# Attention followed by a token mixer: load pieces, a projection's period, the order of the drain and the last store are changed

## The chip, the cores and the metric

The kernel runs on one core of a Trainium2 chip. A core has a matrix engine (TensorE, PE in the profile; PEld is its loading of weights), a vector engine (VectorE, DVE), a scalar engine (ScalarE, ACT), a general one (GpSimd, POOL) and a queue engine (SyncE, SP), which run their own instruction streams in order and wait for each other by semaphores. PE writes to PSUM, an accumulation memory from which DVE or ACT must copy results ("evict" them) to SBUF, the working memory. Sixteen DMA engines move data between HBM (device memory) and SBUF; here POOL issues all loads, which convert float32 to float16 on the way, and SP issues all stores. The metric is the device time of one execution in microseconds, lower is better.

## The reference

```python
def _attn_ref(q, k, v):                  # 8 batches, 8 heads, 576 tokens, head_dim 64
    q_c = q.reshape(B, H, nc, chunk, D)  # chunks of 64 tokens, nc = 9; k_c, v_c alike
    scores = scale * np.matmul(q_c, k_c.transpose(0, 1, 2, 4, 3))
    scores = scores - np.max(scores, axis=-1, keepdims=True)
    attn = np.exp(scores)
    attn = attn / (np.sum(attn, axis=-1, keepdims=True) + 1e-09)
    out = np.matmul(attn, v_c)
...
def _moe_ref(x, w_q, w_k, w_out):        # x: 8 x 576 x 512, the heads side by side
    wq = x @ w_q                         # w_q, w_k: 512 x 64
    wk = x @ w_k
    W_tok = scale * np.einsum('bsd,btd->bst', wq, wk)
    mixed = np.einsum('bst,btd->bsd', W_tok, x)
    return (np.maximum(mixed, 0.0) @ w_out).astype(np.float32)   # w_out: 512 x 512
```

Attention works inside chunks of 64 tokens, so each batch has 72 independent 64 x 64 softmaxes. Its result x goes through a mixer without a softmax, which the kernel computes as wq (wk^T x), so that the token-by-token matrix is never built.

## The kernel before, in words

**Loads.** `load(b, cuts)` fills, for one batch, two tiles `qn` (q and k, 128 partitions x 2 halves of the heads x 9 tiles of tokens) and one tile `vt`. With `cuts` as `None` it issues three DMAs: q, k and v whole, 576 KB each as float16 (L89 to L99). With cuts it issues, for each range of tiles, q in two halves, k in two halves and v in two halves (L100 to L107). Batch 0 is cut in three ranges (18 DMAs, L110), batch 1 in two (12 DMAs, L121). On POOL's queue the projection weights `wqk16` (four DMAs) stand between batch 0 and batch 1, and `wout16` (two DMAs) between batch 1 and batch 2; batches 2 to 5 follow. Batches 6 and 7 are issued from inside the loop when buffers are free.

**Attention.** The 72 chunks of a batch are worked in groups of eight, called units here; 36 units cover the 8 batches, 4.5 units per batch. Unit u goes through stages: `stage_a1` transposes q and k of load tiles 2u and 2u+1 on PE (16 transposes into the one buffer of PSUM tile `tp`, L327); `stage_a2` copies them to `qkt` on DVE (L337); `stage_b1` multiplies q by k (`sp`, L351) and takes the maximum (`mx`, L359); `stage_b2` subtracts it on DVE (`sh`, L365) and takes the exponential on ACT (`es`, L373); `stage_c` transposes that on PE (`ep`, L380) and copies it on ACT (`et`, L382); `stage_d1` multiplies by v (`xp`, L395); `stage_d2` normalises on DVE into `x_nat` (L410).

The order is written out by hand. Period `kk` of the main loop (L453 to L473) issues b1(kk), d1(kk-2), then filler work of place 0, a1(kk+2), filler of place 1, c(kk-1), b2(kk), d2(kk-2), a2(kk+2), filler of place 2. So a1 runs two periods ahead, and every engine meets the work in this order. Before the loop, a1 and a2 of units 0 and 1 are issued.

**The mixer as filler.** `make_moe(b)` makes the steps of batch b. `xts[0..2]` transpose x (six transposes, tile `tx`, L143) and evict them on ACT into `xt` (L150; for the last batch the third is shared by DVE and ACT, L147 and L148). `p_wqk(0)` and `p_wqk(1)` multiply by both projections (`wpa`, `wpb`, L163 and L166; the second also evicts to `wqkT` on ACT, L173 and L174, and copies half of it with DVE, L176). `p_wkn` transposes wk (`wknp`, L190) and evicts it (L195). `p_g` makes wk^T x (`gp`, L205 and L209; evicted on ACT, L213). `p_mixed(0)`, `p_mixed(1)` and `p_mixed_tail` multiply by wq (`ma`, `mb`, L225 and L245) and evict with the ReLU into `rmx` (L131 on ACT; for half of the last batch L129 on DVE). `p_out(0..3)` multiply 128 tokens each by w_out (`op`, four matmuls, L261), evict to `osb` (L269) and store 256 KB through SP (L270); `p_out_tail` does the last 64 tokens (`opt`, eight matmuls, L281, evicted on ACT, L289, and stored in two DMAs, L291). All of these PSUM tiles rotate through the same three buffers.

**The plan.** Each step of `chain` (L298 to L307) is a row (periods after the batch's last unit, place, cost, wait, step). `plan` puts it in that period and place. In a place, `fill` runs the planned steps and then takes ready out steps from `outs` in their order as long as the cost fits a budget (0.7 in place 1, 1.4 or 1.9 in place 2). A batch's outs become ready when its whole chain has run. What the loop does not reach is the drain (L475 to L488): `last` holds the steps of batch 7, `rest` those of earlier batches. It walks both lists with a clock of costs: the next step of batch 7 is issued when `wait` has passed on that clock since the step before it, or nothing else is left; otherwise a step of `rest` or of `outs` is issued. The costs and waits are only numbers that order the instructions; the chip does not see them.

Of the kernel before, what the change touches and what calls it, by code (L numbers as in the profile page):

```python
# [17 lines left out]
def kernel(  # L18
# [15 lines left out]
    nc = tc.nc  # L34
    B, H, S, D = q.shape
    DM = moe_w_out.shape[0]
    DH = moe_w_q.shape[1]
    CH = 64
    P = 128
# [9 lines left out]
    ds = bass.ds  # L49
# [27 lines left out]
    def load(b, cuts):  # L77
        qn = [
            qn_pool.tile([P, 2, NT, R * D], F16, name=f"qn{ti}", tag=f"qn{ti}")
            for ti in range(2)  # L80
        ]
        vt = v_pool.tile([P, 2, NS, D + 2], F16, name="vt", tag="vt")
        flat = [
            x[b].rearrange("h s d -> (h s) d").rearrange("(l t p r) d -> l p t (r d)", l=2, p=P, r=R)
            for x in (q, k)
        ]
        vflat = v[b].rearrange("h s d -> (h s) d").rearrange("(l n p) d -> l p n d", l=2, p=P)
        nc.gpsimd.memset(vt[:, :, :, D : D + 1], 1.0)
        if cuts is None:  # L89
            for ti in range(2):  # L90
                nc.gpsimd.dma_start(
                    qn[ti][:].rearrange("p l t e -> p (l t) e"),
                    flat[ti].rearrange("l p t e -> p l t e").rearrange("p l t e -> p (l t) e"),
                )
            nc.gpsimd.dma_start(  # L95
                vt[:].rearrange("p l n e -> p (l n) e")[:, :, 0:D],
                vflat.rearrange("l p n d -> p l n d").rearrange("p l n d -> p (l n) d"),
            )
            return qn, vt  # L99
        for t0, t1 in cuts:  # L100
            for ti in range(2):
                for sl in range(2):
                    nc.gpsimd.dma_start(qn[ti][:, sl, t0:t1, :], flat[ti][sl, :, t0:t1, :])  # L103
            for sl in range(2):
                nc.gpsimd.dma_start(  # L105
                    vt[:, sl, 2 * t0 : 2 * t1, 0:D], vflat[sl, :, 2 * t0 : 2 * t1, :]
                )  # L107
        return qn, vt

    loads = [load(0, [(0, 2), (2, 5), (5, 9)])]  # L110
    wqk16 = const.tile([P, HQ, 2 * DH], F16, name="wqk16")
    wout16 = const.tile([P, HQ, DM], F16, name="wout16")

    def w_rows(w):
        return w.rearrange("(l i d) j -> l d i j", l=2, i=HQ)

    for sl in range(2):
        rows = slice(CH * sl, CH * sl + CH)
        nc.gpsimd.dma_start(wqk16[rows, :, 0:DH], w_rows(moe_w_q)[sl])
        nc.gpsimd.dma_start(wqk16[rows, :, DH:], w_rows(moe_w_k)[sl])  # L120
    loads.append(load(1, [(0, 3), (3, 9)]))  # L121
    for sl in range(2):
        nc.gpsimd.dma_start(wout16[CH * sl : CH * sl + CH, :, :], w_rows(moe_w_out)[sl])
    for b in range(2, 6):
        loads.append(load(b, None))

    def relu(on_vector, to, of):
        if on_vector:
            nc.vector.tensor_scalar(to, of, scale_moe, 0.0, op0=ALU.mult, op1=ALU.max)  # L129
        else:  # L130
            nc.scalar.activation(to, of, AF.Relu, scale=scale_moe)  # L131

    def make_moe(b):
# [20 lines left out]
        def p_wqk(half):  # L154
            def run():
                xt = st["xt"]
                if half == 0:
                    st["pa"] = m_psum.tile([P, 512], F32, name="wpa", tag="m")
                    st["pb"] = m_psum.tile([P, CH], F32, name="wpb", tag="m")
                pa, pb = st["pa"], st["pb"]  # L160
                for i in (2 * half, 2 * half + 1):
                    flags = dict(start=(i == 0), stop=(i == HQ - 1))
                    nc.tensor.matmul(  # L163
                        pa[:, :], lhsT=wqk16[:, i, :], rhs=xt[:, NC_ * i : NC_ * i + 8, :], **flags
                    )
                    nc.tensor.matmul(  # L166
                        pb[:, :], lhsT=wqk16[:, i, :], rhs=xt[:, NC_ * i + 8, :], **flags
                    )
                if half == 0:
                    return  # L170
                wqkT = moe_pool.tile([P, S], F16, name="wqkT", tag="wqkT")
                wqd = moe_pool.tile([P, S], F16, name="wqd", tag="wqd")
                nc.scalar.copy(wqkT[:, 0:512], pa[:])  # L173
                (nc.vector.tensor_copy if b == B - 1 else nc.scalar.copy)(wqkT[:, 512:S], pb[:])  # L174

                nc.vector.tensor_copy(wqd[CH:P, :], wqkT[0:CH, :])  # L176
                st["wqkT"], st["wqd"] = wqkT, wqd

            return run
# [36 lines left out]
        def p_mixed(w):  # L216
            def run():
                if w == 0:
                    st["rmx"] = moe_pool.tile([P, HQ, S], F16, name="rmx", tag="rmx")
                g16, rmx = st["g16"], st["rmx"]  # L220
                wq = (st["wqkT"][0:CH], st["wqd"][CH:P])
                ms = []
                for par in range(2):
                    ma = m_psum.tile([P, 512], F32, name=f"ma{par}", tag="m")
                    nc.tensor.matmul(  # L225
                        ma[:], lhsT=g16[CH * par : CH * par + CH, w, :], rhs=wq[par][:, 0:512]
                    )
                    ms.append(ma)
                for par in range(2):

                    relu(
                        b == B - 1 and par == 1,
                        rmx[:, 2 * w + par, 0:512].rearrange("p (c g r) -> p c g r", g=G, r=R),
                        ms[par][:].rearrange("p (c r g) -> p c g r", g=G, r=R),
                    )

            return run
# [18 lines left out]
        def p_out(t):  # L256
            def run():
                rmx = st["rmx"]
                op = m_psum.tile([P, DM], F32, name="op", tag="m")
                for i in range(HQ):  # L260
                    nc.tensor.matmul(  # L261
                        op[:],
                        lhsT=rmx[:, i, ds(t * P, P)],
                        rhs=wout16[:, i, :],
                        start=(i == 0),
                        stop=(i == HQ - 1),
                    )
                osb = osb_pool.tile([P, DM], F32, name="osb", tag="osb")
                (nc.vector.tensor_copy if b == B - 1 and t % 2 else nc.scalar.copy)(osb[:], op[:])  # L269
                nc.sync.dma_start(out[b, ds(t * P, P), :], osb[:])  # L270

            return run

        def p_out_tail():
# [20 lines left out]
        xts = [p_xt(g) for g in range(3)]  # L295


        chain = [  # L298
            (1, 2, 0.4, 0.2, xts[2]),
            (1, 2, 0.5, 0.4, p_wqk(0)),  # L300
            (1, 2, 0.5, 0.0, p_wqk(1)),
            (2, 0, 0.4, 1.2, p_wkn),
            (3, 1, 0.7, 0.9, p_g),
            (4, 0, 0.25, 0.8, p_mixed(0)),
            (5, 0, 0.25, 0.8, p_mixed(1)),
            (5, 1, 0.15, 0.5, p_mixed_tail),
        ]  # L307
        outs = [(2, 0.9, p_out(t)) for t in range(4)]
        outs.append((1, 0.5, p_out_tail))
        return xts[:2], chain, outs  # L310

    def batch_of(gj):
# [2 lines left out]
    data = dict(enumerate(loads))  # L315
# [27 lines left out]
    def stage_b1(u):  # L343

        qkt = state[u]["qkt"]
        sp = s_psum.tile([P, 8, CH], F32, name="sp", tag="sp")
        for i in range(8):
            j, c = divmod(i, 4)
            for sl in range(2):
                rows = slice(CH * sl, CH * sl + CH)  # L350
                nc.tensor.matmul(  # L351
                    sp[rows, i, :],
                    lhsT=qkt[rows, j, 0, c, :],
                    rhs=qkt[rows, j, 1, c, :],
                    start=True,
                    stop=True,
                )
        mx = sm_pool.tile([P, 8], F32, name="mx", tag="mx")
        nc.vector.tensor_reduce(mx[:], sp[:], axis=AX.X, op=ALU.max)  # L359
        state[u]["sp"], state[u]["mx"] = sp, mx  # L360
# [72 lines left out]
    outs = []  # L433
# [19 lines left out]
    for kk in range(NU + 2):  # L453
        if kk < NU:
            stage_b1(kk)
        if kk >= 2:
            stage_d1(kk - 2)
        fill(kk, 0, 0.0)
        if kk + 2 < NU:
            stage_a1(kk + 2)  # L460
        fill(kk, 1, 0.7)
        if 1 <= kk <= NU:
            stage_c(kk - 1)
        if kk < NU:
            stage_b2(kk)
        if kk >= 2:
            stage_d2(kk - 2)
        if kk + 2 < NU:
            stage_a2(kk + 2)
        fill(kk, 2, 1.4 if len(outs) < 4 else 1.9)  # L470
        for b in range(B - 6):
            if 4 * (kk - 1) >= NS * (b + 1) > 4 * (kk - 2):
                data[b + 6] = load(b + 6, None)  # L473

    rest = [x for key in sorted(plan) for x in plan[key]]  # L475
    last = [x for x in rest if x[0] == B - 1]
# [40 lines left out]
```

## Time and profile before

| | |
|---|---|
| time, median of 3 runs | 179.73 us (178.91 to 181.5) |
| the profiled execution | 179.23 us |
| its span, first to last instruction | 177.5 us |
| share of that outside of the span | 1.7 us |
| mean granted TensorE clock | 0.98 |
| loads | 14.81 MB as float16, on the software queue |
| stores | 9.44 MB, on the hardware queue |

The profile is one execution. Its page gives for each engine the busy time with its share of the span and the number of instructions, and then the span in 40 equal slices of 4.4 us, one digit each, in tenths of a slice (9 means 90% or more). PEclk is the TensorE clock that was granted, in the same tenths, and DMA the mean busy share of the 16 DMA engines. Lists of waits give who waited for whom, with the total, the number of times and the longest. Timeline rows give start, duration, engine, line, operation, output and inputs, shape and count, and in brackets the idle time of the engine before and what ended it. In the rows that group instructions, what follows the bar is busy time, the mean of one in ns, and the idle time before with what ended it. In the rows of DMA issues, the last number is the time from issue to landing. Busy time of a PE that pipelines its matmuls is modelled and not the same as PE at its peak.

### The profile page before, as it was taken

Reading aid. Unit: us, or ns where it says so; the run is one execution under the profiler, and the core shown is the slowest. Engines: PE = TensorE matmul, PEld = TensorE weight load, DVE = VectorE, ACT = ScalarE, POOL = GpSimd, SP = SyncE. Lnnn points to the kernel's source line nnn. Section 1 sums busy time; section 2 is a strip of 40 time slices with the busy share of each in tenths; the row PEclk is TensorE's granted clock in tenths of the full one; section 3 lists DMA queues with packets and bytes.
Section 4 is the critical chain, followed back from the end, with each engine's and each line's share of the span. In section 5 each row is a group of like instructions: output and inputs, shape, how many; then the busy total and the mean of one; then the engine's idle time right before and its main releaser. Section 6 shows DMA issues by size and latency. Waiting matters only on the chain.

```text
span 177.5 us, 5756 instructions
## 1 busy us (share of the span) xinstructions
PE 140.1 (79%) x2496; PEld 92.2 (52%) x2496; DVE 113.8 (64%) x239; ACT 102.9 (58%) x203; POOL 55.2 (31%) x68
## 2 busy tenths in 40 slices
PE   0364987953977799997997999799979996798990
PEld 0241755842565566665574665566756654454440
DVE  0122869694199778956995988669959865731241
ACT  2001222540548867975797499747956986596630
POOL 8999999916343542422400000000000000000000
PEclk9999999995699999999999999999999999999999
DMA  2999999999999999999999992401303124032435
GB/s 28 98 120 145 112 123 159 185 183 168 177 176 168 182 164 209 231 203 252 178 195 223 173 226 80 151 2 63 94 4 118 60 77 136 0 122 89 177 121 177
DMA packets 82041, 24.62 MB, mean 139 GB/s; under 512 B 76384, under 2 KB 77920, under 8 KB 82016
## 3 DMA queue, kind: packets, MB, share of 16 engines
q0 software_dynamic: 76128, 14.81, 99.1%
q1 hardware_dynamic: 5888, 9.44, 15.5%
q8 instruction: 19, 0.31, 0.7%
q14 instruction: 6, 0.05, 0.1%
HBM read 29.62 MB, written 9.44 MB: 220 GB/s over the span
## 4 chain that ended last, share of the span: by engine, by line
PE 32%; ACT 28%; POOL 17%; DVE 10%; DMA 7%; issue 3%; ACTq 0%; POOLq 0%; DVEq 0%
PE op L261 11%; ACT rmx L131 9%; POOL qn L103 8%; DMA qn<-in_k_dram 7%; ACT xt L150 6%; ACT es L373 5%; POOL vt L105 5%; PE tp L327 4%; PE wpa L163 3%; PE xp L395 2%; ACT et L382 2%; PE ep L380 2%; DVE mx L359 2%; PE sp L351 2%; DVE sh L365 2%
## 5 line engine op out<-in xcount | busy, mean ns | idle before, releaser
L327 PE MATMUL tp<-ident,qn 128*64 128x128 f16 x576 | 30.8, 242 | 17.1 <-DMA qn<-in_q_dram 9.0
L382 ACT COPY et<-ep 128x512 f16<-128x512 f16 x36 | 21.2, 589 | 33.9 <-PE ep L380 33.8
L337 DVE COPY qkt<-tp 128x1024 f16<-128x1024 f16 x36 | 24.6, 682 | 19.1 <-PE tp L327 19.1
L327 PEld LDWEIGHTS <-qn 128*64 128x64 f16 x576 | 21.7, 120 | 25.5 <-DMA qn<-in_q_dram 10.4
L261 PE MATMUL op<-wout,rmx 128*128 128x512 f16 x128 | 31.2, 379 | 0.3 <-ACT xt L148 0.2
L373 ACT ACTIVATE es<-sh 128x512 f16<-128x512 f32 x36 | 22.9, 635 | 13.6 <-DVE sh L365 12.6
L359 DVE TENSOR_REDUCE mx<-sp 128x8 f32<-128x512 f32 x36 | 24.7, 687 | 8.9 <-PE sp L351 8.7
L365 DVE TENSOR_TENSOR sh<-sp,mx 128x512 f32<-128x512 f32 x36 | 24.8, 690 | 2.0
L410 DVE TENSOR_TENSOR x_nat<-xp,rec 128x512 f16<-128x512 f32 x36 | 24.9, 692 | 1.2
L269 ACT COPY osb<-op 128x512 f32<-128x512 f32 x30 | 17.4, 586 | 5.2 <-PE op L261 4.0
L395 PE MATMUL xp<-vt,et 64*64 64x65 f16 x576 | 16.2, 198 | 5.2 <-DVE x_nat L410 3.5
L351 PEld LDWEIGHTS <-qkt 64*64 64x64 f16 x576 | 12.8, 115 | 11.4 <-issue 6.6
L150 ACT COPY xt<-tx 128x768 f16<-128x768 f16 x23 | 18.3, 795 | 0.0
L351 PE MATMUL sp<-qkt 64*64 64x64 f16 x576 | 17.0, 203 | 0.8 <-DVE sh L365 0.8
L131 ACT ACTIVATE rmx<-ma 128x512 f16<-128x512 f32 x30 | 16.5, 610 | 1.2 <-PE ma L225 1.1
L261 PEld LDWEIGHTS <-rmx 128*128 128x128 f16 x128 | 11.6, 98 | 10.4 <-issue 0.2
L395 PEld LDWEIGHTS <-et 64*64 64x64 f16 x576 | 13.0, 113 | 7.3 <-ACT es L373 4.6
L163 PE MATMUL wpa<-xt,wqk 128*128 128x512 f16 x32 | 10.8, 407 | 7.2 <-ACT xt L150 7.2
L95 POOL DMA_DIRECT2D vt<-in_v_dram x6 | 11.0, 1833 | 14.7 <-issue 10.3
L380 PE MATMUL ep<-ident,es 128*128 128x128 f16 x144 | 15.3, 234 | 0.0
L143 PE MATMUL tx<-ident,x_nat 128*128 128x128 f16 x144 | 12.6, 227 | 0.4 <-ACT xt L150 0.3
L176 DVE COPY wqd<-wqkT 64x576 f16<-64x576 f16 x8 | 2.4, 304 | 14.7 <-ACT wqkT L174 14.3
(53 smaller groups left out, 165.8 us busy)
## 6 DMA issues: line engine op xcount, KB each, us to landing
out_dram<-osb SPq DMA_DIRECT2D x32, 256.0 KB, 2.8
qn<-in_q_dram POOLq DMA_DIRECT2D x6, 576.0 KB, 17.1
qn<-in_k_dram POOLq DMA_DIRECT2D x6, 576.0 KB, 18.8
vt<-in_v_dram POOLq DMA_DIRECT2D x6, 576.0 KB, 18.4
out_dram<-osbt SPq DMA_DIRECT2D x16, 64.0 KB, 2.2
wout<-in_moe_w_out_dram POOLq DMA_DIRECT2D x2, 256.0 KB, 8.0
qn<-in_q_dram POOLq DMA_DIRECT2D x4, 96.0 KB, 3.7
qn<-in_k_dram POOLq DMA_DIRECT2D x4, 96.0 KB, 3.5
```

The costliest lines, as they stand in the source:

```text
L131: nc.scalar.activation(to, of, AF.Relu, scale=scale_moe)
L150: nc.scalar.copy(xt[:, 6 * g : 6 * g + 6, :], tx[:])
L261: nc.tensor.matmul(op[:], lhsT=rmx[:, i, ds(t * P, P)], rhs=wout16[:, i, :], start=(i == 0), stop=(i == HQ - 1),)
L327: nc.tensor.transpose(tp[CH * sl : CH * sl + CH, j, ti, :, r, :], src[:, sl, t, r * D : r * D + D], ident[:],)
L337: nc.vector.tensor_copy(qkt[:].rearrange("p j t c k -> p (j t c k)"), tp[:].rearrange("p j t c r g -> p (j t c r g)"),)
L351: nc.tensor.matmul(sp[rows, i, :], lhsT=qkt[rows, j, 0, c, :], rhs=qkt[rows, j, 1, c, :], start=True, stop=True,)
L359: nc.vector.tensor_reduce(mx[:], sp[:], axis=AX.X, op=ALU.max)
L365: nc.vector.tensor_tensor(out=sh[:].rearrange("p i (g r) -> p i r g", g=G, r=R), in0=sp[:].rearrange("p i (r g) -> p i r g", g=G, r=R), in ...
L373: nc.scalar.activation(es[:], sh[:], AF.Exp, scale=scale_attn)
L382: nc.scalar.copy(et[:], ep[:])
L395: nc.tensor.matmul(xv[rows, sl, m, :], lhsT=et[rows, m, CH * sl : CH * sl + CH], rhs=vt[rows, sl, s, 0 : D + 1], start=True, stop=True,)
L410: nc.vector.tensor_tensor(out=x_nat[:, 4 * u : 4 * u + 4, :, :].rearrange("p m l d -> p l m d"), in0=xv[:, :, :, 0:D], in1=rec[:, :, :, No ...
```

## The change

Four things change. First, `load` with cuts now issues only q and k in pieces, in the order half 0 of q, half 0 of k, half 1 of q, half 1 of k, and v always whole, behind them; batch 0 is cut in two ranges, tiles 0 to 3 and 4 to 8 (9 DMAs in place of 18), and batch 1 is not cut (3 in place of 12). Batch 1 is issued ahead of the projection weights, and batch 2 ahead of wout. Second, in the chain `p_wqk` and every step behind it move one period later, `p_wqk` standing one period behind `xts[2]` and no longer in the same place. Third, the waits by which the drain is ordered are other numbers, and for batch 7 the tail out comes ahead of the four outs. Fourth, the last out tile of batch 7 (t = 3) is evicted in two halves, by ACT and DVE, and stored by two DMAs, one issued by ACT and one by SP.

```diff
-        if cuts is None:
+        for t0, t1 in cuts:
+            for sl in range(2):
+                for ti in range(2):
+                    nc.gpsimd.dma_start(qn[ti][:, sl, t0:t1, :], flat[ti][sl, :, t0:t1, :])
+        if not cuts:
             for ti in range(2):
                 nc.gpsimd.dma_start(
                     qn[ti][:].rearrange("p l t e -> p (l t) e"),
                     flat[ti].rearrange("l p t e -> p l t e").rearrange("p l t e -> p (l t) e"),
                 )
-            nc.gpsimd.dma_start(
-                vt[:].rearrange("p l n e -> p (l n) e")[:, :, 0:D],
-                vflat.rearrange("l p n d -> p l n d").rearrange("p l n d -> p (l n) d"),
-            )
-            return qn, vt
-        for t0, t1 in cuts:
-            for ti in range(2):
-                for sl in range(2):
-                    nc.gpsimd.dma_start(qn[ti][:, sl, t0:t1, :], flat[ti][sl, :, t0:t1, :])
-            for sl in range(2):
-                nc.gpsimd.dma_start(
-                    vt[:, sl, 2 * t0 : 2 * t1, 0:D], vflat[sl, :, 2 * t0 : 2 * t1, :]
-                )
+        nc.gpsimd.dma_start(
+            vt[:].rearrange("p l n e -> p (l n) e")[:, :, 0:D],
+            vflat.rearrange("l p n d -> p l n d").rearrange("p l n d -> p (l n) d"),
+        )
         return qn, vt
 
-    loads = [load(0, [(0, 2), (2, 5), (5, 9)])]
+    loads = [load(0, [(0, 4), (4, 9)]), load(1, [])]
...
         nc.gpsimd.dma_start(wqk16[rows, :, DH:], w_rows(moe_w_k)[sl])
-    loads.append(load(1, [(0, 3), (3, 9)]))
+    loads.append(load(2, []))
     for sl in range(2):
         nc.gpsimd.dma_start(wout16[CH * sl : CH * sl + CH, :, :], w_rows(moe_w_out)[sl])
-    for b in range(2, 6):
-        loads.append(load(b, None))
+    for b in range(3, 6):
+        loads.append(load(b, []))
...
                 osb = osb_pool.tile([P, DM], F32, name="osb", tag="osb")
+                if b == B - 1 and t == 3:
+
+                    hw = DM // 2
+                    nc.scalar.copy(osb[:, 0:hw], op[:, 0:hw])
+                    nc.vector.tensor_copy(osb[:, hw:], op[:, hw:])
+                    nc.scalar.dma_start(out[b, ds(t * P, P), 0:hw], osb[:, 0:hw])
+                    nc.sync.dma_start(out[b, ds(t * P, P), hw:], osb[:, hw:])
+                    return
...
         chain = [
-            (1, 2, 0.4, 0.2, xts[2]),
-            (1, 2, 0.5, 0.4, p_wqk(0)),
-            (1, 2, 0.5, 0.0, p_wqk(1)),
-            (2, 0, 0.4, 1.2, p_wkn),
-            (3, 1, 0.7, 0.9, p_g),
-            (4, 0, 0.25, 0.8, p_mixed(0)),
-            (5, 0, 0.25, 0.8, p_mixed(1)),
-            (5, 1, 0.15, 0.5, p_mixed_tail),
+            (1, 2, 0.4, 1.0, xts[2]),
+            (2, 2, 0.5, 0.0, p_wqk(0)),
+            (2, 2, 0.5, 0.0, p_wqk(1)),
+            (3, 0, 0.4, 0.9, p_wkn),
+            (4, 1, 0.7, 0.6, p_g),
+            (5, 0, 0.25, 0.6, p_mixed(0)),
+            (6, 0, 0.25, 0.3, p_mixed(1)),
+            (6, 1, 0.15, 0.3, p_mixed_tail),
         ]
         outs = [(2, 0.9, p_out(t)) for t in range(4)]
-        outs.append((1, 0.5, p_out_tail))
+        outs.insert(0 if b == B - 1 else 4, (1, 0.5, p_out_tail))
```

More of the change, by code (lines that the diff above doesn't have):

```diff
@@ L472 @@
             if 4 * (kk - 1) >= NS * (b + 1) > 4 * (kk - 2):
-                data[b + 6] = load(b + 6, None)
+                data[b + 6] = load(b + 6, [])
     rest = [x for key in sorted(plan) for x in plan[key]]
```

## The prediction

> **What bounds the kernel now.** I read the page first, then the list of what TensorE waited for, then busy time by stretch, then the timeline at the places that these name.
>
> ```profile
> PE 140.1 (79%) x2496; PEld 92.2 (52%) x2496; DVE 113.8 (64%) x239; ACT 102.9 (58%) x203; POOL 55.2 (31%) x68
> PE   0364987953977799997997999799979996798990
> PEclk9999999995699999999999999999999999999999
> DMA  2999999999999999999999992401303124032435
> ```
>
> No engine is full over the span, but the slices differ. In the first ten (4.4 us each) PE is between 0 and 9 and the DMA engines are always full; from the twelfth on PE is at 7 to 9, and the DMA engines empty after slice 24. So there are three stages: a start that loads set, a long middle that PE nearly fills, and a drain.
>
> ```profile
> PE tp L327 <- DMA qn<-in_q_dram: 9.0, 8, 4.2
> PE wpa L163 <- ACT xt L150: 7.2, 7, 1.5
> PE tp L327 <- DMA qn<-in_k_dram: 7.2, 8, 2.9
> PE xp L395 <- DVE x_nat L410: 3.5, 6, 1.2
> ...
> PE wpa L163 <- ACT xt L150: 6.9, 6, 1.5
> ```
>
> Total, times and longest, in us (the last row is the same list for 50 to 157 us alone). PE lost 16.2 us to loads and 7.2 us to one pair of steps: the projection waiting for the eviction of the x transposes just in front of it.
>
> ```profile
> core 0: us, PE busy (x) PEld busy (x) DVE busy (x) ACT busy (x) POOL busy (x), PEclk, DMA share, GB/s
> 4.00:13.00 9.00, 4.36 (x48) 2.71 (x49) 1.38 (x3) 0.00 (x0) 9.00 (x13) 1.00 1.31 106
> 18.00:24.00 6.00, 4.87 (x82) 3.49 (x78) 4.77 (x9) 1.11 (x2) 6.00 (x9) 1.00 1.39 112
> 43.00:47.00 4.00, 3.37 (x28) 2.27 (x29) 0.69 (x1) 1.80 (x3) 1.21 (x1) 0.50 2.22 168
> 64.40:98.70 34.30, 31.25 (x625) 20.89 (x624) 27.40 (x60) 25.74 (x52) 8.36 (x7) 1.00 1.84 209
> ```
>
> While POOL issues small loads (its busy time is the whole window) data comes at 106 to 112 GB/s; with large ones queued it is 168. The last row is nine units (two batches): PE is busy 31.25 of 34.3 us, DVE 27.4, ACT 25.7. So a stall of PE there moves the end.
>
> **Part 1, larger first loads.** Unit u's transposes a1(u) use tiles 2u and 2u+1 of nine per batch, so a1(4) is the first to need batch 1 and a1(9) the first to need batch 2.
>
> ```profile
> 1.48 1.55 POOL L103 DMA_DIRECT2D qn<-in_q_dram  x2
> ...
> 23.88 0.42 PE L327 MATMUL tp<-ident,qn 128*64 128x128 f16 x3 [0.23 <-DMA qn<-in_k_dram]
> ...
> 26.10 1.07 PE L327 MATMUL tp<-ident,qn 128*64 128x128 f16 x16
> ...
> 30.57 0.85 PE L327 MATMUL tp<-ident,qn 128*64 128x128 f16 x11 [0.88 <-DMA qn<-in_k_dram]
> ...
> 36.38 0.64 PE L327 MATMUL tp<-ident,qn 128*64 128x128 f16 x16
> ...
> 40.05 0.30 PE L327 MATMUL tp<-ident,qn 128*64 128x128 f16 x4 [0.70 <-DMA qn<-in_q_dram]
> 43.28 0.85 PE L327 MATMUL tp<-ident,qn 128*64 128x128 f16 x12 [2.93 <-DMA qn<-in_k_dram]
> ```
>
> These are the waits of a1(4), a1(6) and a1(9). After a1(9), no transposes wait for a load any more; so 43.28 us is where the loads let go of the kernel.
>
> ```profile
> qn<-in_q_dram POOLq DMA_DIRECT2D x1, 128.0 KB, 3.4
> ...
> 29.14 1.34 POOL L91 DMA_DIRECT2D qn<-in_q_dram  x1
> 30.36 1.33 POOL L91 DMA_DIRECT2D qn<-in_k_dram  x1
> 31.57 1.94 POOL L95 DMA_DIRECT2D vt<-in_v_dram  x1
> ...
> qn<-in_q_dram POOLq DMA_DIRECT2D x1, 576.0 KB, 10.9
> qn<-in_k_dram POOLq DMA_DIRECT2D x1, 576.0 KB, 12.9
> vt<-in_v_dram POOLq DMA_DIRECT2D x1, 576.0 KB, 15.5
> ```
>
> Issue plus time to landing puts batch 2's three loads at 40.0, 43.3 and 47.1 us: queued large loads land one after another, 3.2 us for q or k and 3.8 for v. A piece of 128 KB lands 3.4 us after issue.
>
> After the change POOL issues four pieces of 128 KB and four of 160 KB (about 0.78 us each, by the 1.55 for two), v of batch 0 whole, then q, k and v of batch 1 whole: about 13 us of issue, ahead of the data from then on. The first piece lands at 1.48+3.4 = 4.9. The other 1024 KB of batch 0's q and k at 3.2 us per 576 KB: 10.6. Then v 14.4, batch 1's q 17.6, its k 20.8. a1(4) now waits for all of that k, where a piece was enough before. This is an added wait: behind it in PE's order stand c(1) and all later units, so DVE and ACT stand too. It ends at about 20.8+0.4 = 21.2, against 24.3 before. The price of a load in this place is bounded below by those 3.2 us and above by the 106 to 112 GB/s of the small pieces; I take the former, because batch 1 now goes as 576 KB loads, like those rows.
>
> From a1(4)'s end to a1(9)'s start took 24.3 to 40.05, of which 0.88 and 0.70 were waits for loads that now have landed: 14.2 us. So a1(9) starts at 35.4. Batch 2's k lands at 20.8 + 3.8 (v) + about 1 (projection weights) + 6.4 = 32, in time. The place that stood at 43.28 after four transposes (0.3 us) stands at 35.7: **-7.6 us**.
>
> Moves that I cost at nothing: v of batch 0 lands at 14.4, and d1(0) comes just ahead of a1(4), which waits longer; projection weights land near 26 and wout near 38, both now behind a batch more, each some 10 us ahead of its first user. If the loads were slower, a1(4) and a1(9) would show it first. The first units start earlier (a1(1) needs no second piece), which only lengthens the stall at a1(4).
>
> Without the gap ahead of 43.28, PE does not run at the 0.50 clock of the 43 to 47 us row. 16 transposes took 1.07 us in the early stretch and 0.64 later; of the 3.37 us of PE in that window the slow share is at most 0.4 of it: **-1.3 us**. The new stall, about 5 us before 21, falls where PE was slow anyway (1.07 at 26.1). The Trainium skill (TensorE: Matmul & The Clock Gate, Part 1: The HAM clock gate) says that the array runs at half rate until it has been kept busy for some 3.4 us, and falls back after an idle window as long; the gaps of 0.70 and 2.93 us with 0.50 behind them agree. By it PE would be at full speed from about 25 us, where the trace shows slow transposes until about 33; that would take perhaps 1 us more off, to 163.7.
>
> **Part 2, projections a period later.** No instruction is added. xts[2] keeps its period, p_wqk and all behind it move by one.
>
> ```profile
> 95.94 0.38 PE L163 MATMUL wpa<-xt,wqk 128*128 128x512 f16 x1 [1.04 <-ACT xt L150]
> ...
> 149.55 0.38 PE L163 MATMUL wpa<-xt,wqk 128*128 128x512 f16 x1 [1.52 <-ACT xt L150]
> ```
>
> With a period of some 3.5 us between them, the eviction (behind et and es on ACT) is done long before. Bounds: nothing (or a new wait of the same size), and the whole 6.9 us of the six waits after 50 us. I take all of it, **-6.9 us**, since PE is 91% busy in that stretch and the next engine has 7 us of slack in 34.3. Late next are the two wqkT copies on ACT ahead of p_wkn; they keep their distance of one place. The three shared PSUM buffers turn over in the same manner, and no wait is added on SP or POOL.
>
> **Part 3, the drain.** By the plan's numbers, mixed(0) of batch 6 and the out tail of batch 5 no longer fit in the loop. The loop loses their matmuls, two and eight (about 0.4+0.6 us): **-1.0 us**. The drain now runs mixed(0), mixed(1), tail of batch 6 and the tail out of batch 5 ahead of batch 7's xts[2].
>
> ```profile
> 156.53 0.37 PE xp L395 x16
> ...
> 160.30 0.47 ACT xt L148
> ...
> 173.33 0.37 ACT osbt L289
> ...
> L269 ACT COPY osb<-op 128x512 f32<-128x512 f32 x6 | 3.5, 586 | 4.6 <-PE op L261 3.8 <-ACT rmx L131 0.8
> L131 ACT ACTIVATE rmx<-ma 128x512 f16<-128x512 f32 x6 | 3.3, 610 | 0.1
> L289 ACT COPY osbt<-opt 128x256 f32<-128x256 f32 x3 | 1.1, 374 | 1.0 <-PE opt L281 1.0
> L131 ACT ACTIVATE rmx<-mb 128x128 f16<-128x128 f32 x3 | 0.7, 281 | 0.0
> ...
> 173.99 1.13 SPq L291 DMA_DIRECT2D out_dram<-osbt  x2
> ...
> out_dram<-osb SPq DMA_DIRECT2D x9, 256.0 KB, 2.0
> out_dram<-osbt SPq DMA_DIRECT2D x6, 64.0 KB, 2.0
> ```
>
> Before, batch 7's last eviction starts 3.8 us after the last xp and the last eviction of all at 16.8. After, g and out(3) of the batches before stand in the last period, and then ACT evicts out(3) 0.59, four rmx 2.4, two mb 0.56 and osbt 0.37, some 3.9 us, from the end of out(3) (about 2.7 after xp); with three PSUM buffers the transposes wait for these. So xts[2] is evicted near 6.6: 2.8 later. From there PE is filled by the same outs, so all 2.8 counts. The last tile in halves costs 0.37, as the 256-wide osbt does; two queues issue one store each instead of SP two (1.13): 0.5 less. Drain **+2.3 us**; bounds 0 (if the waits on the chain that the fillers now cover give it back) and +4 (all evictions ahead).
>
> **Sum.** -7.6 -1.3 -6.9 -1.0 +2.3 = -14.5. The profiled execution took 179.2 us (span 177.5); the median is 179.7. So 164.7.
>
> **Rivals.** A, slow first loads: batches 0 and 1 up to k (2.95 MB) at 106 to 112 GB/s land at about 30, not 20.8. Then a1(9) is at 44.6, 9 us later: 173.9. For it: those rates; against: they hold where POOL is busy all the window, which it no longer would be.
> B, the stall moves: the evictions come no earlier, and ACT or DVE become the bound in the full periods: part 2 gives nothing, 171.6. For it: periods are uneven, and DVE needs 3 us of each unit; against: the slack above.
> C, loads bounded by issue alone: k of batch 1 lands some 3.4 us after its issue at about 11.3, a1(4) goes on near 16, 5.2 us earlier: 159.5. The rows at 40.0, 43.3 and 47.1 speak against it. The Trainium skill (DMA: Bandwidth & Descriptors, Anatomy of one DMA) gives about 2.0 us plus the bytes at 436 GB/s, 1.35 us for such a load; the trace has 3.2.
> D, slower: the 5 us stall leaves the clock at half speed into the middle. At 1.07 for 0.64, PE's 31.25 us of nine units become 52, up to 2.3 us per unit; it decides from 8 units on, with 18 us lost: above 183. Against: 1.00 all through 64 to 98 us, although PE had stopped for 2.93 us at 40.
>
> **How the numbers follow.** The likeliest, 0.69, is the sum, with 161 to 168.5 as its own range (loads -1 to +2, part 2 up to +3, drain -2.3 to +1.7). A 0.10, B 0.13, C 0.05, D 0.03. Range 159.5 to 172.5: it takes in B and C and leaves out D and most of A. About 2% (below 176.1, above 183.3) can be told from no change. A, B, C and the sum all lie below 176 but for A's upper end: faster 0.90, same 0.06, slower 0.04.
>
> **What would show it.** Part 1: a1(4) waiting once for batch 1's k until 21 or 22, no wait at a1(9), and no 0.50 clock near 43. Part 2: the list of PE's waits without wpa, and nine units in about 32 us. Part 3: batch 7's last xt eviction 6 to 7 us after the last xp. Wrong would be: a1(4) near 30 (A), a new wait of 1 us per batch (B), or a drain from last xp of over 25 us (21 now).

## The result, and the profile after

| kernel | median, us (range) | ratio to before, 95% interval |
|---|---|---|
| before | 179.47 (178.91 to 181.50) | |
| after | 170.01 (168.71 to 172.95) | 0.943 (0.931 to 0.955) |

The change takes 9.5 us off, where 14.5 were predicted: 170.0 us lies inside the range given, 159.5 to 172.5, and above the 161 to 168.5 of the likeliest case. The execution profiled at 172.95 us was a disturbed one, so the profile shown here is a second one of the same kernel (169.62 us, span 167.5 us).

Rows of the page of the kernel after: busy time, two of the rows of 40 slices (4.2 us each), and the queue that brings instructions (packets, MB, share).

```profile
PE 135.8 (81%) x2496; PEld 89.8 (54%) x2496; DVE 113.4 (68%) x239; ACT 102.4 (61%) x204; POOL 44.0 (26%) x50
...
PE   0178249677799999999969999999999988979690
...
PEclk9999999999978999999996999999999999999999
...
q8 instruction: 19, 0.31, 0.7%
```

From the twelfth slice to the 32nd PE is at 9 with one exception, where it was at 7 to 9 before. The exception is the 21st slice with a 6, and in the slice behind it the granted clock falls. The 19 packets of q8 are 16 KB each.

What PE waited for in the kernel after (total, times, longest, us):

```profile
PE tp L330 <- DMA qn<-in_q_dram: 9.9, 3, 4.7
...
PE tp L330 <- DMA qn<-in_k_dram: 3.2, 2, 2.6
PE ep L383 <- issue: 1.6, 1, 1.6
```

The projection's wait for the x transposes (7.2 us before) is gone from the list, as forecast. In its place stands a single wait of 1.6 us with no releaser: PE stood still for nothing that the profile shows.

Busy time by stretch in the kernel after, under the same heads as before:

```profile
core 0: us, PE busy (x) PEld busy (x) DVE busy (x) ACT busy (x) POOL busy (x), PEclk, DMA share, GB/s
95.33:126.65 31.32, 30.73 (x625) 20.68 (x624) 27.39 (x59) 25.46 (x54) 0.00 (x0) 1.00 0.45 100
84.36:92.08 7.72, 5.87 (x72) 2.90 (x70) 4.07 (x9) 4.76 (x11) 0.00 (x0) 0.79 1.84 202
3.00:12.00 9.00, 3.35 (x52) 2.50 (x53) 1.57 (x3) 0.00 (x0) 9.00 (x11) 1.00 1.56 144
16.00:23.00 7.00, 1.64 (x28) 1.12 (x28) 2.35 (x5) 0.54 (x2) 3.10 (x4) 1.00 1.96 178
44.50:47.90 3.40, 1.96 (x58) 1.62 (x56) 3.30 (x7) 1.15 (x2) 2.07 (x2) 0.99 2.21 170
47.90:51.30 3.40, 3.40 (x52) 2.15 (x46) 2.52 (x7) 2.17 (x4) 1.22 (x1) 0.51 2.23 169
85.40:88.80 3.40, 1.58 (x28) 1.11 (x27) 2.73 (x6) 1.91 (x5) 0.00 (x0) 1.00 1.78 220
88.80:92.20 3.40, 3.40 (x16) 1.16 (x16) 0.30 (x1) 1.82 (x5) 0.00 (x0) 0.50 1.79 191
```

The first row is nine units: 31.32 us, against 34.3 before. The second is one period, that from unit 21 to unit 22: 7.72 us, of which PE was busy for 5.87, part of it at half clock.

The timeline of PE in the kernel after, at the loads and around that period:

```profile
20.16 0.42 PE L330 MATMUL tp<-ident,qn 128*64 128x128 f16 x4 [2.80 <-DMA qn<-in_q_dram]
23.23 0.42 PE L330 MATMUL tp<-ident,qn 128*64 128x128 f16 x4 [2.64 <-DMA qn<-in_k_dram]
...
25.45 1.06 PE L330 MATMUL tp<-ident,qn 128*64 128x128 f16 x16
...
28.10 0.64 PE L330 MATMUL tp<-ident,qn 128*64 128x128 f16 x16
...
37.06 0.64 PE L330 MATMUL tp<-ident,qn 128*64 128x128 f16 x16
...
84.36 0.44 PE L354 MATMUL sp<-qkt 64*64 64x64 f16 x16
...
88.35 0.38 PE L383 MATMUL ep<-ident,es 128*128 128x128 f16 x4 [1.60 <-issue]
...
92.08 0.48 PE L354 MATMUL sp<-qkt 64*64 64x64 f16 x16
...
118.85 0.44 PE L354 MATMUL sp<-qkt 64*64 64x64 f16 x16
...
123.45 0.44 PE L354 MATMUL sp<-qkt 64*64 64x64 f16 x16
```

a1(4) waits for batch 1's q until 20.16 us and then for its k until 23.23; a1(9) starts at 37.06 and waits for nothing. The period with the standstill takes 7.72 us, the same period of the plan two batches later 4.60 (118.85 to 123.45).

Where the time went, from the same three marks in both profiles (the span, us; the last x_nat ends at 158.07 before and at 144.99 after):

| stretch | before | after | change | predicted |
|---|---|---|---|---|
| to a1(9), behind its first four transposes | 43.28 | 37.17 | -6.1 | -7.6 |
| from there to the end of the last x_nat | 114.8 | 107.8 | -7.0 | -1.3 -6.9 -1.0 = -9.2 |
| from there to the end | 19.4 | 22.5 | +3.1 | +2.3 |
| span | 177.5 | 167.5 | -10.0 | -14.5 |

### The profile page after: what moved, and what is told of

Read it like the earlier page. It is cut to its first block, busy times and chain, and to the rows that moved or that the text cites. A ratio compares the mean times of both kernels' runs of the same rounds, so it can differ in the third digit from the quotient of the medians.

```text
span 170.8 us, 5751 instructions
## 1 busy us (share of the span) xinstructions
PE 137.1 (80%) x2496; PEld 90.7 (53%) x2496; DVE 113.8 (67%) x239; ACT 102.6 (60%) x204; POOL 44.1 (26%) x50
## 4 chain that ended last, share of the span: by engine, by line
PE 50%; DVE 17%; ACT 12%; DMA 8%; POOL 6%; issue 4%; ACTq 0%; DVEq 0%; POOLq 0%
PE op L256 15%; DMA qn<-in_k_dram 8%; PE tp L330 6%; PE ep L383 5%; ACT rmx L126 4%; DVE sh L368 4%; PE xp L398 4%; DVE x_nat L413 4%; PE sp L354 4%; PE wpa L158 4%; POOL qn L92 4%; DVE mx L362 3%; DVE qkt L340 3%; PE tx L138 3%; PE opt L284 2%
## 5 line engine op out<-in xcount | busy, mean ns | idle before, releaser
L330 PE MATMUL tp<-ident,qn 128*64 128x128 f16 x576 | 27.5, 239 | 15.3 <-DMA qn<-in_q_dram 9.6
L340 DVE COPY qkt<-tp 128x1024 f16<-128x1024 f16 x36 | 24.5, 682 | 16.6 <-PE tp L330 16.6
L256 PE MATMUL op<-wout,rmx 128*128 128x512 f16 x128 | 33.2, 392 | 0.4 <-ACT osb L272 0.4
L330 PEld LDWEIGHTS <-qn 128*64 128x64 f16 x576 | 20.7, 119 | 21.0 <-DMA qn<-in_q_dram 10.3
L376 ACT ACTIVATE es<-sh 128x512 f16<-128x512 f32 x36 | 22.8, 634 | 11.1 <-DVE sh L368 10.9
L99 POOL DMA_DIRECT2D vt<-in_v_dram x8 | 14.7, 1835 | 18.2 <-issue 11.3
L383 PEld LDWEIGHTS <-es 128*128 128x128 f16 x144 | 8.8, 102 | 5.9 <-issue 3.5
L95 POOL DMA_DIRECT2D qn<-in_k_dram x7 | 8.6, 1228 | 12.8 <-issue 10.0
```

The source lines that it names most:

```text
L256: nc.tensor.matmul(op[:], lhsT=rmx[:, i, ds(t * P, P)], rhs=wout16[:, i, :], start=(i == 0), stop=(i == HQ - 1),)
L330: nc.tensor.transpose(tp[CH * sl : CH * sl + CH, j, ti, :, r, :], src[:, sl, t, r * D : r * D + D], ident[:],)
L340: nc.vector.tensor_copy(qkt[:].rearrange("p j t c k -> p (j t c k)"), tp[:].rearrange("p j t c r g -> p (j t c r g)"),)
L376: nc.scalar.activation(es[:], sh[:], AF.Exp, scale=scale_attn)
L383: nc.tensor.transpose(ep[:, m, :], es[:, 2 * m : 2 * m + 2, :], ident[:])
```

## The experiments

The theories after the result: the load term is short because batch 1's k lands later than worked out; the middle is short because of the standstill; the drain is long for the reason predicted. The rivals: the pieces themselves, rather than the wait for the whole of k, eat the gain; the standstill comes from data or loads; and the drain is set by ACT's left-over evictions and the halved tile, rather than by the start of the chain.

**The kernel after once more** (no edit).

> The changed kernel unaltered, for a second profile. In the first one, unit 21 to 22 took 8.0 us where the same place of the pattern took 4.6 to 5.1 nine units before and after, with PE standing 1.9 us for no shown reason and a half clock behind it. Theory: that is no part of the kernel. Expected: 168.5 to 169.5 us, that period at 4.6 to 5.1 us; batch 1's k lands near 24.3 us again, and the drain (last x_nat to the end) takes 23 to 24 us again, with a half clock in it. Rival: the standstill is a cost of the moved steps and shows in the same place again.

169.94 us (168.51 to 170.31), 0.943 (0.935 to 0.950). The profile above is of this run. The time is 0.4 us above what was expected. The theory fell and the rival held: the standstill is there again, at the same transposes, with 1.60 us (1.87 in the first profile), and the period takes 7.72 us (8.03). Batch 1's k came sooner than expected, at 23.2 us, and the drain took 22.5 us without half clock in it; in the first profile it was 23.8 us with 3.4 us of half clock.

**The loads alone.** The chain's rows, the outs' order and the last tile are as before; `load` and the order of the loads as after.

```diff
-            (2, 2, 0.5, 0.0, p_wqk(0)),
+            (1, 2, 0.5, 0.4, p_wqk(0)),
...
-        outs.insert(0 if b == B - 1 else 4, (1, 0.5, p_out_tail))
+        outs.append((1, 0.5, p_out_tail))
```

> The kernel before with part 1 alone: the changed load function, cuts and order of the loads; plan, drain and last store as before. By the sum of the prediction (a1(9) at 35.7 us, -7.6, and -1.3 for the clock): 170.3 us. By the profile of the changed kernel (batch 1's k lands at 24.3, not 20.8, and the place after a1(9)'s first four transposes is at 38.7, so -4.6, and -1.3): 173.4 us.

**The plan, drain and last tile alone.** The loads are as before.

```diff
-    loads = [load(0, [(0, 4), (4, 9)]), load(1, [])]
+    loads = [load(0, [(0, 2), (2, 5), (5, 9)])]
...
-    loads.append(load(2, []))
+    loads.append(load(1, [(0, 3), (3, 9)]))
```

> The kernel before with parts 2 to 4 alone: the chain a period later behind the x transposes, the waits of the drain, the place of the tail out and the last store in halves; loads as before. By the prediction (-6.9 -1.0 +2.3): 173.6 us. By the profile of the changed kernel (loop -8.6, drain +4.4): 175.0 us. No wait of the projections for the x eviction in the list; drain from the last x_nat about 23.5 us against 19.4.

The loads alone took 174.57 us (0.970, 0.961 to 0.979), the rest alone 174.27 us (0.968, 0.960 to 0.976). Beside the 180.0 of the kernel before, measured with them, that is 5.4 and 5.7 us, together 11.1, against 10.1 for both: the two add up nearly. The loads alone saved less than either sum expected (170.3 and 173.4 us); the plan alone lies between its two (173.6 and 175.0), with the drain at 22.5 us. The waits of PE with the loads alone hold the projection's wait as before:

```profile
PE wpa L158 <- ACT xt L145: 8.0, 7, 1.5
```

With the plan alone, PE waits for loads as before, and the standstill is there too (timeline of PE):

```profile
43.42 0.85 PE L335 MATMUL tp<-ident,qn 128*64 128x128 f16 x12 [3.20 <-DMA qn<-in_k_dram]
...
89.20 0.44 PE L359 MATMUL sp<-qkt 64*64 64x64 f16 x16
...
93.47 0.28 PE L388 MATMUL ep<-ident,es 128*128 128x128 f16 x2 [1.65 <-issue]
...
96.50 0.63 PE L359 MATMUL sp<-qkt 64*64 64x64 f16 x16
```

It falls in the same step, 5.1 us later in time: with the old loads behind 2754 records of PE (matmuls, weight loads and the waits of its sequencer counted together), with the new ones behind 2753. So it goes with the place in the new plan's instructions, under either order of the loads, and not with the clock time. Whether it hangs on what is done there or on the count of instructions is tried below. With the loads alone there is none.

**Batch 0 whole.** Are the pieces what delays batch 1's k?

```diff
-    loads = [load(0, [(0, 4), (4, 9)]), load(1, [])]
+    loads = [load(0, []), load(1, [])]
```

> The changed kernel with batch 0's q and k loaded whole too, no pieces at all. Theory (the eight pieces are what runs slower than 3.2 us per 576 KB, since POOL needs 0.9 us of issue for 160 KB): batch 1's k lands near 21 us, a1(4) and a1(9) come 3 us earlier, 166 us. Rival (the early loads are late with or without pieces, because a DMA counts as landed when the slowest DMA engine is done, and that one lags from the start): k lands near 24 us again, 169 us.

168.92 us (0.930, 0.918 to 0.941): not the 166 of the theory, and not clearly less than the kernel after. Batch 1's k comes 1.4 us sooner (timeline of PE):

```profile
21.85 0.42 PE L330 MATMUL tp<-ident,qn 128*64 128x128 f16 x4 [1.12 <-DMA qn<-in_k_dram]
```

So the pieces cost something over 1 us of the 2.4 by which k was late (23.2 for 20.8). The rest is in the rate of the first loads whatever their size: with this kernel 138 GB/s from 3 to 8 us and 184 from 16 to 21.

**Batch 1 in pieces again.** Is the added wait the price?

```diff
-    loads = [load(0, [(0, 4), (4, 9)]), load(1, [])]
+    loads = [load(0, [(0, 4), (4, 9)]), load(1, [(0, 3), (3, 9)])]
```

> The changed kernel with batch 1's q and k in pieces again (tiles 0 to 2 and 3 to 8), v whole. If a1(4) is late because the change makes it wait for the whole of batch 1's k: its last wait ends near 19.5 us, not 23.2 to 24.4, and a1(9) then waits for batch 2's k, near 35.7 for 37.2; in all about 168. Rival (pieces run slower, so that what a1(4) gains is lost behind it): a1(9) no earlier than 37 us, 169.5.

167.76 us (0.928, 0.921 to 0.935). The timeline of PE:

```profile
18.59 0.42 PE L330 MATMUL tp<-ident,qn 128*64 128x128 f16 x3 [0.17 <-DMA qn<-in_k_dram]
...
34.63 0.85 PE L330 MATMUL tp<-ident,qn 128*64 128x128 f16 x12 [1.80 <-DMA qn<-in_k_dram]
```

a1(4) is past its loads at 19.0 rather than 23.6 us. a1(9) then waits 1.8 us for batch 2's k, and the place behind its first four transposes stands at 34.6, 2.5 us earlier than after; the time is 2.2 us less. Beside the 43.28 us of the kernel before, that place comes 8.7 us earlier, where 7.6 were predicted. So leaving batch 1 uncut is what cost the loads a part of their gain. The rival, that the pieces lose behind a1(4) what they gain there, falls.

**Sixteen more transposes.** In period 2, behind d1(0), 16 transposes of the identity are added that nothing reads. They move all later instructions of PE by 32 (each has a weight load).

```diff
+        if kk == 2:
+            extra = et_psum.tile([P, 4, P], F16, name="ep", tag="ep")
+            for n in range(16):
+                nc.tensor.transpose(extra[:, n % 4, :], ident[:], ident[:])
```

> The changed kernel with 16 more transposes of the identity on PE (32 instructions, a result that nothing reads) in the stall ahead of a1(4). Two questions. First, all three kernels with the new plan stand still at the same PE instruction, the transposes of unit 20's softmax, whatever their loads. If that belongs to a place in PE's instruction stream (its supply), 32 instructions more move or remove it: the period from unit 21 to 22 falls from 7.7 to 4.6 to 5.1 us, in all 166.5 us. If it belongs to what is done there, it stays at 7.3 to 8.4 us. Second, the extra work keeps PE busy for 5 us: if the clock rises after some 3.4 us of work, the transposes behind a1(4) take 0.64 us and not 1.06; units of the start took 2.86 us slow and 3.03 us fast, so that no time should come of it.

168.84 us (0.938, 0.931 to 0.945). The timeline of PE:

```profile
25.31 1.06 PE L330 MATMUL tp<-ident,qn 128*64 128x128 f16 x16
...
80.34 0.41 PE L200 MATMUL gp<-x_nat,wkn 128*64 128x256 f16 x4 [1.12 <-issue]
...
85.23 0.44 PE L354 MATMUL sp<-qkt 64*64 64x64 f16 x16
...
89.83 0.44 PE L354 MATMUL sp<-qkt 64*64 64x64 f16 x16
```

The period from unit 21 to unit 22 is 4.60 us here, as it is two batches later. But the standstill is not gone: it stands 256 records earlier, at another instruction (`gp`), with 1.12 us, and one of 0.6 us is new. Counted over all fourteen profiles, every pause of PE over 0.1 us without a releaser lies at one place of a group of 256, 193 or 194 records behind a multiple of 256 (962, 1218, 1474, 1729, 2241, 2497, 2753 and 3265, give or take one), and neither the kernel before nor the one with the loads alone has any. The transposes behind a1(4) still took 1.06 us: the added work did not bring the full clock to them. Nor did the 166.5 us come that a period of 4.60 was to give: from a1(9) to the last x_nat this profile is 1.8 us shorter than the kernel after, as other pauses stand in for the one that moved, and its drain is 1.3 us longer, with half clock from 147.9 to 151.3 us.

**The drain with the chain first.** The wait of `xts[2]` is 0, so that batch 7's transposes stand ahead of what is left of batch 6.

```diff
-            (1, 2, 0.4, 1.0, xts[2]),
+            (1, 2, 0.4, 0.0, xts[2]),
```

> The changed kernel with the wait number of xts[2] at 0.0 in place of 1.0, so that batch 7's x transposes and projections come first in the drain, ahead of what is left of batch 6. The prediction's account of the drain (its chain starts 2.8 us later, and all of that counts): the time from the last x_nat to the end falls from 22.5 us to 19.7, in all 167 us for 169.5. Rival (what counts is that ACT has to evict the left-over steps of batch 6, wherever they stand): the transposes come some 3 us earlier, but the next steps then wait behind the same evictions, and the drain stays within 0.7 us of 22.5.

**Half of batch 6's evictions on DVE.** The relus of one half go to DVE for the last two batches, not for the last alone.

```diff
-                        b == B - 1 and par == 1,
+                        b >= B - 2 and par == 1,
...
-                    b == B - 1 and par == 1,
+                    b >= B - 2 and par == 1,
```

> The changed kernel with half of batch 6's ReLU evictions (which all lie in the drain) on DVE instead of ACT, as batch 7's are. If ACT's evictions at the start of the drain set its length: ACT has two rmx and one mb less, 1.4 us, and the drain from the last x_nat falls from 22.5 to about 21.1 us. Rival (PE's own work sets it): no change, 22.5.

Chain first: 170.26 us (0.943, 0.935 to 0.952), no difference from the kernel after. DVE: 168.50 us (0.936, 0.928 to 0.944). The timelines of three drains, first that of the kernel after:

```profile
144.30 0.69 DVE L413 TENSOR_TENSOR x_nat<-xp,rec 128x512 f16<-128x512 f32 x1
...
146.47 2.07 ACT L126 ACTIVATE rmx<-ma 128x512 f16<-128x512 f32 x4
...
150.09 0.48 ACT L143 COPY xt<-tx 128x384 f16<-128x384 f16 x1 [0.46 <-DVE xt L142]
...
151.83 0.40 PE L185 MATMUL wknp<-ident,wqkT 64*128 64x64 f16 x8
```

then the chain first:

```profile
146.12 0.69 DVE L413 TENSOR_TENSOR x_nat<-xp,rec 128x512 f16<-128x512 f32 x1
...
148.49 0.48 ACT L143 COPY xt<-tx 128x384 f16<-128x384 f16 x1
...
149.92 2.07 ACT L126 ACTIVATE rmx<-ma 128x512 f16<-128x512 f32 x4
...
152.60 0.40 PE L185 MATMUL wknp<-ident,wqkT 64*128 64x64 f16 x8
```

and the relus on DVE:

```profile
144.23 0.69 DVE L413 TENSOR_TENSOR x_nat<-xp,rec 128x512 f16<-128x512 f32 x1
...
149.33 0.48 ACT L143 COPY xt<-tx 128x384 f16<-128x384 f16 x1 [0.46 <-DVE xt L142]
...
151.06 0.40 PE L185 MATMUL wknp<-ident,wqkT 64*128 64x64 f16 x8
```

From the last x_nat, the last eviction of `xt` starts 5.8 us later in the kernel after, 2.4 with the chain first. But `wknp`, three steps down the chain, gains 1.0 of those 3.4 us (7.5 to 6.5): PE issues it behind the tail of batch 6, which waits for batch 6's relus, and these stand on ACT behind `xt` and `wqkT` now. ACT's evictions have only changed places. The time does not change. With the relus on DVE, `wknp` comes 0.7 us sooner, and the stretch from the last x_nat to the end is 21.84 us, 0.67 less than 22.51: half of what was expected, of the expected sign. In the profile with the chain first, half clock from 153.1 to 156.5 lengthens the drain, so its length (24.5) tells nothing further. Half clock fell into the drain of three more profiles of this plan (the first of the kernel after, the sixteen transposes and the two tiles), and it took 23.8 us in each; the 22.5 us are without it.

**The last tile whole.** The lines with the halves are taken out.

```diff
-                if b == B - 1 and t == 3:
...
-                    nc.scalar.copy(osb[:, 0:hw], op[:, 0:hw])
-                    nc.vector.tensor_copy(osb[:, hw:], op[:, hw:])
...
-                    return
```

> The changed kernel with the last out tile evicted whole by DVE and stored by one DMA, as before. By the prediction the halves save about 0.5 us (0.2 of eviction, the rest by the store). By the profile of the changed kernel DVE's half waits until ACT's half is done, so the halves take as long as the whole: from the last matmul to the end 4.5 us in both, within 0.3.

**The halves in two SBUF tiles.**

```diff
+                    osc = osb_pool.tile([P, DM], F32, name="osb", tag="osb")
...
-                    nc.vector.tensor_copy(osb[:, hw:], op[:, hw:])
+                    nc.vector.tensor_copy(osc[:, hw:], op[:, hw:])
```

> The changed kernel with the two halves of the last out tile written to two SBUF tiles instead of one. DVE's half started only when ACT's was done. If that is because both write one tile: now they run together, and from the last matmul to the end it takes 4.1 us, not 4.5. Rival (both read one PSUM tile, and that orders them): DVE still waits, 4.5.

Whole: 168.96 us (0.940, 0.932 to 0.949). Two tiles: 170.29 us (0.937, 0.929 to 0.946). The timelines of the last evictions, of the kernel after:

```profile
163.09 0.37 ACT L267 COPY osb<-op 128x256 f32<-128x256 f32 x1 [0.28 <-PE op L256]
...
163.50 0.42 DVE L268 COPY osb<-op 128x256 f32<-128x256 f32 x1 [1.43 <-ACT osb L267]
```

of the whole tile:

```profile
162.67 0.69 DVE L264 COPY osb<-op 128x512 f32<-128x512 f32 x1 [1.03 <-PE op L256]
```

and of two tiles:

```profile
164.91 0.42 DVE L269 COPY osb<-op 128x256 f32<-128x256 f32 x1 [1.50 <-ACT osb L268]
```

DVE does not start beside ACT: it waits for ACT's half, so the halves take 0.83 us (163.09 to 163.92) where one copy takes 0.69. With separate SBUF tiles it still waits; what is left in common is the PSUM tile that both read. From the end of the last matmul to the end of the span it is 4.49 us with halves, 4.55 with two tiles and 3.98 whole, where 4.5 was expected for the whole tile too. Of these 0.5 us the eviction is only 0.13. The other 0.4 lie behind the last landing of a store: from there to the end of the span it is 0.91 us whole and 1.33 with halves. In all five profiles in which SP issues every store it is 0.89 to 0.96, in the nine in which ACT issues one it is 1.32 or more. That ACT's store is the cause is not shown, since halves stored by SP alone were not run. The medians lie within each other's ranges; the 0.5 us is read from the profiles.

**Three together, without and with sixteen transposes.** Batch 0 whole, batch 6's relus shared with DVE, the last tile whole; the second has 16 transposes of the identity besides, ahead of everything else, which nothing reads.

```diff
-    loads = [load(0, [(0, 4), (4, 9)]), load(1, [])]
+    loads = [load(0, []), load(1, [])]
...
-                    b == B - 1 and par == 1,
+                    b >= B - 2 and par == 1,
...
+    extra = et_psum.tile([P, 4, P], F16, name="ep", tag="ep")
+    for n in range(16):
+        nc.tensor.transpose(extra[:, n % 4, :], ident[:], ident[:])
```

> The changed kernel with three of the edits at once: batch 0 loaded whole, half of batch 6's ReLUs on DVE, the last tile stored whole. From their own runs: a1(9) 1.2 us earlier, drain 0.7 and 0.5 shorter: 167.0 us against 169.5. PE's instructions up to the drain are the same as in the changed kernel, so by the theory of the instruction stream the standstill at the same instruction remains, period 21 to 22 at 7 us or more.

> The same three edits, with 16 transposes of the identity on PE ahead of everything (32 instructions, a result that nothing reads), while PE waits for the first load. If the standstill hangs on where the instruction lies in PE's stream: period 21 to 22 at 4.6 us, smaller standstills elsewhere at records that differ from the 2753rd by a multiple of 256, and about 2 us less than without them: 165 us. Rival (the earlier gain came from the place of the extra work in the stall): 167, as without them.

166.89 us (0.923, 0.916 to 0.930) without and 166.85 us (0.926, 0.921 to 0.932) with them: both faster than the kernels before and after, and equal to each other. The first is as expected (167.0). The 2 us expected of the sixteen did not come. Batch 1 in pieces as well was not run with them. The timeline of PE without them:

```profile
84.14 0.44 PE L346 MATMUL sp<-qkt 64*64 64x64 f16 x16
...
88.40 0.38 PE L375 MATMUL ep<-ident,es 128*128 128x128 f16 x4 [1.87 <-issue]
...
90.56 0.44 PE L346 MATMUL sp<-qkt 64*64 64x64 f16 x16
```

and with them, where the period from unit 21 to unit 22 takes 4.60 us:

```profile
79.75 0.49 PE L200 MATMUL gp<-x_nat,wkn 128*64 128x256 f16 x5 [1.15 <-issue]
```

Without them the standstill of 1.87 us has no half clock behind it in this profile, so its period is 6.42 us, not 7.72 (7 or more was expected). Moving the standstill then saves little, since 1.15 us of it stands in another period.

## Why the prediction was right or wrong

The direction and the three places were right, and about two thirds of the size. That 170.0 us lies inside the range is in part luck: the range was drawn to 172.5 to take in rival B, which did not happen, and the sum's own range ended at 168.5.

**Loads, -7.6: measured -6.1.** The mechanism held: all the waiting at a1(4), none at a1(9). The term was mis-sized where the landings were summed up: at 3.2 us per 576 KB from 4.9 us on, batch 1's q was to land at 17.6 us and its k at 20.8; they landed at 20.2 and 23.2. The step from q to k was right (3.1 us), so the whole delay arose ahead of q's landing: the pieces came at 144 GB/s (3 to 12 us), where 3.2 us per 576 KB is 184, and the large loads behind them at 178. From a1(4) to a1(9) it was then 0.9 us shorter than worked out, which gave some back. Batch 0 whole and batch 1 cut show each share.

**Clock, -1.3: measured nothing.** With the loads alone the stretch from a1(9) to the last x_nat took 115.25 us, before 114.8. The gap at a1(9) went, as said, but the half clock came later, from 47.9 to 51.3 in the kernel after. The failed step is that without the gap PE would not run at half clock: in the 3.4 us ahead of that, DVE was busy for 3.30 and PE for only 1.96. In the kernel before it was alike: there the clock fell at 40.7 us, 0.4 us into the gap of 2.93, behind

```profile
37.30:40.70 3.40, 1.23 (x37) 0.82 (x36) 3.23 (x8) 1.12 (x2) 0.34 (x1) 1.00 1.82 185
```

so the gap that the prediction took for the reason came mostly behind the fall. The transposes behind a1(4) took 1.06 us at 25.45 and 0.64 at 28.10; from unit 3's `sp` to unit 4's it was 2.86 us and from unit 6's to unit 7's, at full clock, 3.03, so the slow clock there cost no time that these rows show. By the rule of the Trainium skill (TensorE: Matmul & The Clock Gate, Part 1: The HAM clock gate), as the prediction used it, full clock was to come near 25 us; it came by 28, as a1(4) went on 2.4 us later than reckoned.

**Projections, -6.9, and the loop, -1.0: more than that, and then 3.1 lost.** The wait left the list and nine units took 31.32 us, 3.0 less than before, where 2.3 were predicted ("about 32"). Without the long period the middle would have given 10.1 us in place of 7.9. The standstill with its half clock took back 3.1 (7.72 for 4.60). It was in no term and in none of the rivals: rival B had a stall that moves, but to evictions and in each batch, and no such wait is in the list. This is the largest part of the miss.

**Drain, +2.3: measured +3.1** (and +4.4 in the profiles with half clock in the drain). In the chain of the kernel after, the last xp starts at

```profile
143.45 0.37 PE xp L398 x16
```

and the last eviction of `xt` (150.09) 6.6 us later, as forecast (6 to 7). But the step "so all 2.8 counts" fell: with 3.4 us of that delay undone, the time stayed. That ACT's left-over evictions count, in whatever order, is supported by the run that gives half of them to DVE, at half the size expected. And the last tile, put at 0.5 less than before, came out 0.3 more: from the end of the last matmul to the end of the span it was 4.17 us before and is 4.49 after. The saving by the store came (2.86 us from the last eviction to the last landing before, 2.25 after). But the halves do not overlap, so the last eviction ends 0.91 us behind the last matmul in place of 0.41, and from the last landing to the end it is 1.33 us in place of 0.90. That 0.8 is the whole miss in this term.

In sum, 14.5 became 10.0 of span: 1.5 from the loads, 1.3 from the clock, 3.1 from the standstill, 0.8 from the drain, less 2.2 by which the middle gained more. None of the four rivals happened.

## What to carry to other kernels

Where several loads are queued, cut the one that the next stage waits for, even if pieces cost rate: a whole load that stands later in a kernel at no cost can be the one wait of the start. When an engine is brought to 98% busy (30.73 of 31.32 us), a new limit can show that no wait between engines names, so look for "issue" in the list of waits and count at which instruction it falls. Splitting the last eviction between two engines pays only if the trace shows them side by side, and the stretch behind the last landing belongs to the comparison.

## What the runs showed of the hardware

**A standstill bound to the place in PE's instructions.** The q8 queue moves 16 KB at a time, about once per 256 records of PE. In the kernel after, while loads run, PE reached the next such place 2.2 to 2.8 us after the start of such a transfer, nine groups running; in the kernel before it was 2.9 to 8.6 us. The transfer ahead of the standstill began at 86.2 us, 7.8 after the one before it (6.4 to 7.0 at the seven before that), when PE had four records left; PE went on at 88.35. That its instructions came late is thus what the numbers suggest; it is not shown. Why the transfer started late there, and whether the loads, the last of which lands at 102 us, hold it up, was not tried. The Trainium skill (Runtime: NRT & Kernel Launch, Instruction fetch mechanics) says that instructions are streamed in blocks of 16 KiB, 256 instructions, and that crossing a boundary is "mostly hidden". The spacing agrees; under this plan one crossing cost 1.1 to 1.9 us.

**Half clock after a stretch that was only partly idle.** In the windows of the kernel after, the granted clock falls to 0.51 behind 3.4 us in which PE was busy for 1.96, and to 0.50 behind 1.58. Read in the same manner over fourteen profiles, each of the 31 falls (those at the very end left aside) followed 3.4 us with PE busy for 0.3 to 2.6 us, and each rise followed at least 2.96. Between 1.5 and 2.6 both outcomes occur. With batch 0 whole, DVE relus and the last tile whole, the standstill was shared by two such stretches (2.44 and 2.27 us busy), and no fall came. The Trainium skill (TensorE: Matmul & The Clock Gate, Part 1: The HAM clock gate) has the same length, 3.4 us, but names an idle window for the fall; here a window half busy was enough.
